# Turned exponentials through memory: where the permutation is done, at the store or at the load

## The chip, the cores and the metric

One core of one Trainium2 chip runs the whole program in one launch. The metric is the device time of an execution in microseconds (us). A profiled execution also has a span: the time from its first to its last recorded instruction. Engine names in the rows are those of the profile: PE is TensorE, PEld its weight loads, DVE is VectorE, ACT is ScalarE, POOL is GpSimd, SP is SyncE. A q behind a name is that engine's queue, where it issues DMAs.

## The reference

The program is local attention followed by a gated feed-forward layer.

```python
# q, k, v: (8, 8, 576, 64); heads 0-3 see a plain window of 32, heads 4-7 every 4th of 128
scores = np.matmul(q, k.transpose(0, 1, 3, 2)) / np.sqrt(64)
scores = np.where(masks[None], scores, -1e9)
attn = np.exp(scores - scores.max(-1, keepdims=True))
attn = attn / (attn.sum(-1, keepdims=True) + 1e-9)
y = np.matmul(attn, v)
# x: the heads of a token side by side, (4608, 512)
g = x @ w_gate                                   # 512 -> 1536
out = (g / (1 + np.exp(-g)) * (x @ w_val)) @ w_out   # 1536 -> 512
```

## The kernel before

**Feed-forward.** The 4608 tokens are nine chunks of 512. The first three go through plain products; the other six are taken two by two (NCS = 3 pairs) through seven products of half-size blocks in place of eight (NT = 7, the names of the loops at lines 1171 to 1206). In each pair a stage of gate and value products comes first (6 blocks of 7 products, each product in two groups of 6 matmuls, one into bank `bg` or a `bo` and one into `bv` or a `bo`), then a stage of output products. Every fp32 operand is split in a high and a low part, so each product takes three matmuls. The mixed weights of the seven products are kept in device memory as `pieces` and come back in loads of 512 KB through a ring of seven (`next_piece`, line 996). A finished product is either kept by ACT (`keep`, line 1071) or summed by DVE (`total`, line 1075), which frees its bank of PSUM.

**Attention.** It is cut in 38 packs (`packs`, line 125). A pack has 2 x 4 x 4 blocks of 32 queries by 64 keys. Its steps run beside the feed-forward work, three visits to a pack, at slots given by `visits` (line 854) and carried out by `attend` (line 878):

- Visit A: the results of an earlier pack (`results`, line 625) and this pack's scores (`scores`, line 552) on TensorE, both into the two banks `two`; then `norm` (line 636) and `turn_y` (line 654) of the earlier pack, and `shift` (line 572) and `exps` (line 589) of this one. Then the loads: keys and queries, values, and, from pack 20 on, `load_far` (line 618) of the pack before.
- Visit B: the exponentials are turned, so that keys lie on partitions. Up to pack 19 TensorE does it (`turn_e`). From pack 20 on (TURNED) `turn_far` (line 610) does it: DVE transposes every block of 32 x 32 into a tile `x`, which is stored to the memory buffer `turned` (two of them, used in turn), and `load_far` loads it into the tile `pt`. The blocks still have to be put in order, 4 by 4, and that is done by the pattern of the transfers.
- Visit C: the results are put where the feed-forward work takes its input (`x_copies`).

For these 18 packs, the exponentials of pack m are stored after its visit B, loaded at visit A of pack m + 1, and used by TensorE at visit A of pack m + 2 (`ended`, line 873).

In the stage of these packs the rings of `later` (line 517) have one buffer each: `e`, `y` and `pt` of one tile each. `norm` writes its result into `y`, and `turn_far` its transposed blocks too.

**What sets the order.** Everything behind the start is recorded by the class Desk (line 155) and issued in an order that Desk.issue plans; the order of TensorE's work stays as written, that of the other engines is planned. Desk.places (line 184) says which blocks of memory an instruction touches: of on-chip memory the columns, without regard to partitions; of a DRAM tile the number of a 128 x 1024 block, which is 0 for all of `turned`. An instruction that writes blocks is planned behind the last writer and the readers of them (`used`, line 209). A DMA is planned with 430 ns at its issue, its bytes at 373 per ns and 2000 ns to land, and counts one instruction behind another as late as that. Its priority is its way, the length of the chain behind it:

```python
    LANDING, RATE, AHEAD = 2000, 373, 2000
    EARLY = 6000
    ...
            cost, later = 430, self.LANDING + nbytes(out) / self.RATE
    ...
            way[k] = cost + later + (self.EARLY if later and e == 'scalar' else 0) + max((way[m] for m in after[k]), default=0)
```

The real waits on the chip are put in by the framework; the plan only gives each engine its order.

Of the kernel before, what the change touches and what calls it, by code (L numbers as in the profile page):

```python
# [34 lines left out]
BQ = 32  # L35
# [40 lines left out]
NH = 4  # L76
# [251 lines left out]
def attention_moe(ctx, tc, qkb, vb, w, const, out):  # L328
    nc = Desk(tc.nc)
# [33 lines left out]
    turned = [tc.dram_tile([P, P * NG], F32, name=f"turned{n}") for n in range(2)]  # L363
# [246 lines left out]
    def turn_far(m, pool):  # L610


        x = pool["y"]()
        e = st[m]["e"].rearrange("q (g b k) -> q b g k", g=NG, b=4)
        nc.vector.transpose(out=x.rearrange("q (b g k) -> q b g k", b=4, g=NG), in_=e)
        nc.sync.dma_start(out=turned[m % 2], in_=x)

    def load_far(m, pool):
        t = pool["pt"]()
        far = turned[m % 2].rearrange("(j k) (b x) -> b k j x", b=4, j=NH)  # L620
        for b in range(4):
            nc.scalar.dma_start(out=t[BQ * b:BQ * b + BQ].rearrange("k (j x) -> k j x", j=NH), in_=far[b])
        st[m]["pt"] = t

    def results(m, two):
# [183 lines left out]
    for n, x in enumerate(MASKS[:4]):  # L809
        nc.vector.tensor_copy(out=mask_sb[:, BK * n:BK * n + BK], in_=two_masks[:, BK * "Fo".index(x):][:, :BK])  # L810
    nc.vector.tensor_copy(out=mask_sb[:, 4 * BK:].rearrange("q (g k) -> q g k", k=BK),
                          in_=two_masks[:, BK:].unsqueeze(1).broadcast_to([P, NM - 4, BK]))
# [65 lines left out]
    def attend(now):  # L878
        for what, m in visit.get(now, ()):
            r = ended(m)  # L880
            if what == "A":
# [14 lines left out]
                if 2 * NSTART <= m < TURNED:  # L896
                    load_v(m, later, nc.sync)
                elif TURNED <= m - 1 < NPK:
                    load_far(m - 1, later)
                    load_v(m - 1, later, nc.sync)  # L900
                if 2 * NSTART <= m + 1 < NPK:
                    load_qk(m + 1, later, nc.sync)
            elif what == "B":
                if TURNED <= m < NPK:
                    turn_far(m, later)
                elif m < NPK:
                    turned_at = bank_o[3] if m == BEFORE - 1 else two[:, 1]
                    turn_e(m, turned_at)
                    keys(m, turned_at, pool_of(m))
            elif r is not None:  # L910
                x_copies(r)
# [342 lines left out]
```

## Time and profile before

| | us |
|---|---|
| median of 3 runs | 910.74 (910.35 to 911.76) |
| the profiled execution | 911.71 |
| its span | 909.9 |
| TensorE busy | 898.7 (99%) |
| DVE busy | 651.9 (72%) |
| ACT busy | 382.3 (42%) |
| POOL busy | 261.0 (29%) |

The granted clock of TensorE has a mean of 0.996 of its full speed. Busy shares are read first, then the waits of the engine that is busiest; matmuls are pipelined and their ends are modelled, so gaps between starts say more than idle time. The 18 stores into `turned` are issued between 333.2 and 656.2 us, the 72 loads from it between 335.7 and 671.2 us. The DMA-issuing instructions of a queue are not counted as busy time of its engine.

### The profile page before, as it was taken

Reading aid. Unit: us, or ns where it says so; the run is one execution under the profiler, and the core shown is the slowest. Engines: PE = TensorE matmul, PEld = TensorE weight load, DVE = VectorE, ACT = ScalarE, POOL = GpSimd, SP = SyncE. Lnnn points to the kernel's source line nnn. Section 1 sums busy time; section 2 is a strip of 40 time slices with the busy share of each in tenths; the row PEclk is TensorE's granted clock in tenths of the full one; section 3 lists DMA queues with packets and bytes.
Section 4 is the critical chain, followed back from the end, with each engine's and each line's share of the span. In section 5 each row is a group of like instructions: output and inputs, shape, how many; then the busy total and the mean of one; then the engine's idle time right before and its main releaser. Section 6 shows DMA issues by size and latency. Waiting matters only on the chain.

```text
span 909.9 us, 20899 instructions
## 1 busy us (share of the span) xinstructions
PE 898.7 (99%) x8642; PEld 737.2 (81%) x8642; DVE 651.9 (72%) x993; ACT 382.3 (42%) x593; POOL 261.0 (29%) x177
## 2 busy tenths in 40 slices
PE   7999999999999999999999999999999999999998
PEld 4988888888888888888888888787878888888886
DVE  6889779978795473777789767878687746555752
ACT  5887423332333242333345533432445533334452
POOL 2479612212211121111132620111046501213451
PEclk9999999999999999999999999999999999999999
DMA  9999976545374641888887778888866675565562
GB/s 347 367 342 343 371 266 236 178 153 181 117 268 143 206 137 39 279 277 275 283 289 263 227 246 296 293 285 270 274 215 217 214 243 192 190 203 186 193 223 93
DMA packets 90382, 214.24 MB, mean 235 GB/s; under 512 B 9264, under 2 KB 32432, under 8 KB 90288
## 3 DMA queue, kind: packets, MB, share of 16 engines
q1 hardware_dynamic: 79776, 208.09, 66.9%
q10 hardware_dynamic: 10512, 4.82, 2.0%
q8 instruction: 68, 1.11, 0.5%
q14 instruction: 26, 0.21, 0.1%
HBM read 165.69 MB, written 47.19 MB: 234 GB/s over the span
## 4 chain that ended last, share of the span: by engine, by line
PE 92%; DMA 4%; DVE 2%; ACT 1%; issue 0%; SPq 0%; ACTq 0%; DVEq 0%
PE bo L251 42%; PE bv L251 22%; PE bg L251 22%; PE two L251 6%; DMA at_float<-turned 2%; DVE at_float L251 1%; DMA at_int<-w 1%; DMA at_float<-qkb 1%; ACT at_int L251 0%; ACT at_float32r L251 0%; SPq L235 0%; DVE at_int L251 0%; DVE at_float32r L251 0%; ACT at_float L251 0%; ACT at_int L235 0%
## 5 line engine op out<-in xcount | busy, mean ns | idle before, releaser
L251 PE MATMUL bo<-at_float32r 128*128 128x512 f32 x1296 | 305.5, 390 | 0.0
L251 PEld LDWEIGHTS bo<-at_float32r 128*128 128x128 f32 x1296 | 242.6, 188 | 50.9
L251 POOL TENSOR_TENSOR at_float32r<-at_float,at_float32r 128x512 fp32r<-128x512 f32 (+1 forms) x109 | 161.3, 1483 | 392.3 <-ACT at_float32r L251 236.2
L251 ACT CAST at_float32r<-at_float 128x512 fp32r<-128x512 f32 (+2 forms) x214 | 147.4, 705 | 162.8 <-DVE at_float L251 72.5
L251 DVE TENSOR_TENSOR at_float<-bo,at_float 128x512 f32<-128x512 f32 x168 | 114.2, 684 | 99.8 <-ACT at_float L251 63.5
L251 DVE TENSOR_TENSOR at_float32r<-at_float,at_float32r 128x512 fp32r<-128x512 f32 (+1 forms) x105 | 109.0, 1052 | 55.2 <-ACT at_float32r L251 43.8
L251 PE MATMUL bv<-at_float32r 128*128 128x512 f32 x486 | 128.5, 391 | 0.0
L251 PE MATMUL bg<-at_float32r 128*128 128x512 f32 x486 | 128.2, 390 | 0.0
L251 ACT ACTIVATE at_float<-at_float 128x512 f32<-128x512 f32 (+1 forms) x108 | 67.9, 630 | 133.4 <-DVE at_float L251 111.9
L251 POOL TENSOR_TENSOR at_float<-at_float,at_float 128x512 f32<-128x512 f32 x36 | 51.2, 1423 | 211.3 <-DVE at_float L251 210.3
L251 PE MATMUL bg<-at_float32r,at_float32r 128*128 128x512 f32 (+1 forms) x468 | 108.9, 381 | 1.5 <-POOL at_float32r L235 0.9
L251 PE MATMUL bv<-at_float32r,at_float32r 128*128 128x512 f32 (+1 forms) x468 | 108.0, 380 | 0.0
L251 DVE SCALAR_TENSOR_TENSOR at_float<-at_float,at_float 128x512 f32<-128x512 f32 x144 | 106.3, 744 | 1.1
L251 PE MATMUL bo<-at_float32r,at_float32r 128*128 128x512 f32 (+1 forms) x468 | 106.5, 376 | 0.0
L251 PEld LDWEIGHTS bg<-at_float32r 128*128 128x128 f32 x486 | 90.9, 188 | 19.1
L251 PEld LDWEIGHTS bv<-at_float32r 128*128 128x128 f32 x486 | 90.7, 188 | 19.2
L251 PEld LDWEIGHTS bg<-at_float32r,at_float32r 128*128 128x128 f32 x468 | 83.2, 190 | 18.7 <-POOL at_float32r L235 1.3
L251 PEld LDWEIGHTS bv<-at_float32r,at_float32r 128*128 128x128 f32 x468 | 83.7, 192 | 16.5 <-DVE at_float L251 0.6
L251 PEld LDWEIGHTS bo<-at_float32r,at_float32r 128*128 128x128 f32 x468 | 82.8, 188 | 16.3
L251 ACT COPY at_float<-bg 128x512 f32<-128x512 f32 x63 | 37.0, 587 | 84.9 <-PE bg L251 81.0
L251 DVE TENSOR_TENSOR at_float<-at_float,at_float 128x512 f32<-128x512 f32 (+2 forms) x80 | 63.9, 808 | 2.4 <-POOL at_float L251 1.2
L251 ACT COPY at_float<-bv 128x512 f32<-128x512 f32 x63 | 37.1, 589 | 36.8 <-PE bv L251 35.3
(74 smaller groups left out, 620.4 us busy)
## 6 DMA issues: line engine op xcount, KB each, us to landing
at_float32r<-pieces SPq DMA_DIRECT2D x189, 512.0 KB, 4.2
pieces<-at_float32r SPq DMA_DIRECT2D x126, 256.0 KB, 4.4
at_float<-qkb SPq DMA_DIRECT2D x32, 576.0 KB, 6.4
at_float<-vb SPq DMA_DIRECT2D x34, 520.0 KB, 5.3
at_int<-w SPq DMA_DIRECT2D x38, 384.0 KB, 6.0
out<-at_float SPq DMA_DIRECT2D x36, 256.0 KB, 4.4
turned<-at_float SPq DMA_DIRECT2D x18, 256.0 KB, 4.7
at_float<-turned ACTq DMA_DIRECT2D x72, 64.0 KB, 5.0
```

What stands on the lines that cost most here:

```text
L251: self.kept.append([engine, lambda: f(*a, **k), sorted(m for m in after if m >= 0), cost, later, both, start])
```

## The change

The store of the transposed tile becomes four stores, one for each group of 32 partitions, which write the blocks of 128 elements where they belong in `turned`. The four loads, one for each group of 32 partitions of `pt`, become one plain load of the whole tile. The bytes are the same: 256 KB each way. The contiguous run is 2048 bytes in the old store and the new load, 512 bytes in the old loads and the new stores. The stores are issued by SP and the load by ACT, as before.

```diff
         x = pool["y"]()
         e = st[m]["e"].rearrange("q (g b k) -> q b g k", g=NG, b=4)
         nc.vector.transpose(out=x.rearrange("q (b g k) -> q b g k", b=4, g=NG), in_=e)
-        nc.sync.dma_start(out=turned[m % 2], in_=x)
+        far = turned[m % 2].rearrange("(b k) (j x) -> j k b x", b=4, j=NH)
+        for j in range(NH):
+            nc.sync.dma_start(out=far[j], in_=x[BQ * j:BQ * j + BQ].rearrange("k (b x) -> k b x", b=4))
 
     def load_far(m, pool):
         t = pool["pt"]()
-        far = turned[m % 2].rearrange("(j k) (b x) -> b k j x", b=4, j=NH)
-        for b in range(4):
-            nc.scalar.dma_start(out=t[BQ * b:BQ * b + BQ].rearrange("k (j x) -> k j x", j=NH), in_=far[b])
+        nc.scalar.dma_start(out=t, in_=turned[m % 2])
         st[m]["pt"] = t
```

## Rows read from the trace of the kernel before

**Rows 1.** Page, part 1: engine, busy us (share of span), instructions.

```profile
PE 898.7 (99%) x8642; PEld 737.2 (81%) x8642; DVE 651.9 (72%) x993; ACT 382.3 (42%) x593; POOL 261.0 (29%) x177
```

**Rows 2.** Busy us (instructions) in stretches; then granted clock, DMA share, GB/s.

```profile
355.00:470.00 115.00, 115.00 (x1292) 94.27 (x1291) 81.53 (x137) 42.24 (x70) 15.59 (x12) 1.00 0.80 265
...
550.00:685.00 135.00, 133.25 (x1605) 108.70 (x1591) 106.48 (x178) 52.24 (x87) 24.24 (x18) 1.00 0.82 270
```

**Rows 3.** Waits of PE, 320 to 680 us: total us, times, longest.

```profile
PE two L251 <- DMA at_float<-turned: 1.8, 4, 0.7
```

**Rows 4.** Timeline of PE, first matmul of six passes and first behind: start, us.

```profile
563.00 0.81 PE L251 MATMUL two<-at_float,at_float 64*32 64x65 f32 x60
...
564.43 0.96 PE L251 MATMUL bo<-at_float32r 128*128 128x512 f32 x3
...
576.89 0.30 PE L251 MATMUL two<-at_float,at_float 64*32 64x65 f32 x2
...
578.94 0.73 PE L251 MATMUL bo<-at_float32r 128*128 128x512 f32 x2
...
619.20 0.30 PE L251 MATMUL two<-at_float,at_float 64*32 64x65 f32 x2
...
621.60 0.96 PE L251 MATMUL bo<-at_float32r 128*128 128x512 f32 x3
...
634.07 0.89 PE L251 MATMUL two<-at_float,at_float 64*32 64x65 f32 x60
...
635.57 0.73 PE L251 MATMUL bv<-at_float32r 128*128 128x512 f32 x2
...
648.04 0.30 PE L251 MATMUL two<-at_float,at_float 64*32 64x65 f32 x2
...
649.89 0.97 PE L251 MATMUL bo<-at_float32r 128*128 128x512 f32 x3
...
662.36 0.30 PE L251 MATMUL two<-at_float,at_float 64*32 64x65 f32 x2
...
663.97 0.98 PE L251 MATMUL bv<-at_float32r 128*128 128x512 f32 x3
```

**Rows 5.** Timeline of ACT, 563 to 573 us (ACTq: DMA issues).

```profile
563.89 0.84 ACTq L251 DMA_DIRECT2D at_float<-turned  x2
...
568.84 0.59 ACT L251 COPY at_float<-bg 128x512 f32<-128x512 f32 x1 [0.59 <-PE bg L251]
568.85 0.31 ACTq L251 DMA_DIRECT2D at_float<-turned  x1
...
572.72 0.31 ACTq L251 DMA_DIRECT2D at_float<-turned  x1
```

**Rows 6.** DMAs, 330 to 680 us: queue's packets, MB, share; issues, KB, us to landing.

```profile
q10 hardware_dynamic: 10368, 4.72, 5.2%
...
turned<-at_float SPq DMA_DIRECT2D x18, 256.0 KB, 4.7
at_float<-turned ACTq DMA_DIRECT2D x72, 64.0 KB, 5.0
```

**Rows 7.** Timeline of SP's queue, 556 to 576 us.

```profile
556.95 0.32 SPq L251 DMA_DIRECT2D turned<-at_float  x1
...
570.72 0.32 SPq L251 DMA_DIRECT2D turned<-at_float  x1
572.91 3.04 SPq L251 DMA_DIRECT2D at_float32r<-pieces  x2
```

**Rows 8.** Timeline of DVE, 581 to 585 us.

```profile
581.08 0.68 DVE L251 TENSOR_TENSOR at_float<-two,at_float 128x512 f32<-128x512 f32 x1
...
582.63 0.69 DVE L251 TENSOR_TENSOR at_float<-bo,at_float 128x512 f32<-128x512 f32 x1
583.68 0.71 DVE L251 STREAM_TRANSPOSE at_float<-at_float 128x512 f32<-128x512 f32 x1 [0.36 <-ACT at_float L251]
```

## Prediction, before any run of the changed kernel

> **What bounds the kernel now.** I read the page's busy shares first: TensorE is busy for nearly the whole span [rows 1]. The table of stretches then says the same of the two stretches where the changed transfers run, 355 to 470 us and 550 to 685 us: the first shows no idle TensorE at all, the second 1.75 us in 135 [rows 2]. So work taken off another engine is worth nothing by itself; only a wait of TensorE can be won. The list of TensorE's waits has one entry there: the passes into `two` waited four times for loads from `turned`, 1.8 us in all [rows 3].
>
> That list counts idle time only, and matmul ends are modelled, so I priced the waits from the timeline by starts. A pass that waits for nothing takes 1.43 us from its first matmul at 563.00 to the first matmul behind it at 564.43 [rows 4]. Five others, all in the second stretch, take 2.05, 2.40, 1.50, 1.85 and 1.61 us [rows 4]. Their excess is 0.62 + 0.97 + 0.07 + 0.42 + 0.18 = 2.26 us. **That is all the change can win.**
>
> Why the loads are late is seen on ACT: two of one pack's loads go out from 563.89, the third at 568.85, the fourth at 572.72 [rows 5]; with the 5.0 us median of such a load [rows 6] the fourth would land at 577.7, and its pass begins at 576.89 [rows 4]. The spreading is the planner's: Desk.places looks at columns, not partitions, so the four loads, which write the same columns of `pt`, count as a chain of writers (0.43 + 2.00 + 0.18 = 2.61 us each, lines 164 and 243), and other ACT work is put between them. The three gaps add up to 572.72 - 563.89 = 8.83 us, 2.94 each.
>
> **The change part by part.** *Four loads become one.* ACT issues three fewer DMAs in each of 18 packs, at 0.31 us each [rows 5], some 17 us of queue time on an engine busy under 40% of these stretches [rows 2]: nothing, since ACT is not what TensorE waits for. The chain of four goes. One load of 256 KB has the store's size, 4.7 us, against 5.0 us for 64 KB [rows 6]; I take 4.7.
>
> *One store becomes four.* SP issues three more DMAs, 3 x 0.32 us a pack [rows 7], beside piece loads that wait for TensorE anyway: 0. Packets of 512 bytes move from the load to the store. The loads' queue shows 10368 packets in 5.2% of 16 engines over 350 us, 28 ns each [rows 6]; 512 of these over 16 engines are 0.9 us, taken off one side and put on the other: 0.
>
> *The chain moves to SP.* To the planner the whole `turned` buffer is one block (line 193), so the four stores now count as a chain of writers, and the load waits for the last. Before shows no such store; the bounds are 0.32 us between stores (issued back to back [rows 7]) and 4.7 us (each waits until the one before has landed [rows 6]). I take 2.94 us, the gap that the same chaining rule gave the loads. It also is close to the 2.72 us between two piece loads on SP (a pair fills 3.04 us, less 0.32 of the second issue [rows 7]), and pieces are what will stand between the stores.
>
> *Does the load come in time?* Take the tightest pack: store at 556.95 [rows 7], pass at 576.89 [rows 4], 19.94 us. After the change: 3 x 2.94 to the last store, 4.7 to its landing, 4.7 for the load: 18.2 us. It lands 1.7 us ahead, so the 2.26 us go. The ends: back to back, 10.4 us, 9.6 us ahead; with 4.7 us gaps 23.5 us, 3.6 us late.
>
> *The wait it adds.* `y` is a single buffer in this stage (line 517): turn_far's transposed tile and norm's result share it. Norm's multiply on DVE ran at 581.08 [rows 8], and the store of 570.72 [rows 7] had landed by 575.4: 5.7 us to spare. The last of four stores goes out at 570.72 + 8.83 = 579.55 and lands at 584.25: the multiply would be held 3.2 us. The planner knows of the dependence and moves the multiply to 579.55 + 2.61 = 582.16 in its plan, so 2.1 us of hold are left. Behind it on DVE stand the total of a bank (582.63) and the next pack's transpose (583.68) [rows 8]; ACT is held likewise at the load, for 2.1 us, with the copies from `bg` and `bv` behind it. Who waits for them? TensorE, when it writes the bank again. After the copy of 568.84, 0.59 us [rows 5], there are three groups of six matmuls (half of 2.72 each) before the bank is due: over 3 us, enough. The tight one is product 4: kept by ACT (0.59), then the total on DVE (0.69 [rows 8]), with one product (2.72) before its bank is written: 1.44 us of margin, once in seven products or 19 us. A 2.1 us hold falls on it in 2.1/19 = 11% of 18 packs, two packs, and costs at most 2.1 - 1.44 = 0.66 us: 0 to 1.3 us, I take 0.6. The lower end is no cost: what follows is then hidden by the margin. A gain is excluded, since nothing here gets `y` earlier.
>
> *Priorities.* The planner adds 6 us of urgency to each ACT load in a chain (line 263). Four chained loads and the store gave 4 x 8.61 + 3.13 = 37.6 us, now it is 4 x 2.61 + 9.13 = 19.6 us. Transposes and exponentials of these packs lose 18 us of urgency and may run a little later on DVE, which has 28 us idle in 135 [rows 2]. TensorE's order is fixed. I take 0 within the 1.7 us that the load is ahead.
>
> *A rule against the split.* The trace shows 64 KB landing no sooner than 256 KB, 5.0 and 4.7 us [rows 6]. The Trainium skill, "DMA: Bandwidth & Descriptors", Rules for kernel authors, asks for one transfer over all partitions, as split ones serialize and small ones are mostly overhead; the trace agrees on the overhead, and no row shows the serializing. By it four stores would follow each other at 4.7 us, the late end above, instead of 2.94.
>
> **The sum.** Of the profiled execution: 911.71 - 2.26 + 0.6 = 910.05, say 910.0 us. That execution is 0.97 us above the median of the runs, 910.74; if this scatter sits in the same waits, the median run has only some 1.3 us of them to lose, and 910.0 is 0.7 us below it, 0.08%. A measurement of this kernel tells about 0.2%, 1.8 us, from no change.
>
> **The rivals.** *All of it is gained.* The scatter lies elsewhere (the start, where transfers bound), every run loses the 2.26 us, and the holds fall on margins: 910.74 - 2.26 = 908.5. For it: the waits have one cause, which goes. Against: it needs the holds to cost nothing. Chance 0.20.
>
> *Nothing is gained.* The waits of the five passes stay or come back, since pieces between the stores push the load out by the 1.7 us: 911.0, the median with the 0.3 us of half a hold. Chance 0.11.
>
> *Slower by the one `y` buffer.* The stores spread so that the multiply is held the full 3.2 us, or more. It decides from the point where a hold passes 1.44 us and meets product 4. At 3.2 us it meets it in 3.2/19, one pack in six, three of 18, costing 1.76 us each, 5.3 us: 909.45 + 5.3 = 914.7. If it met it in every pack, 909.45 + 18 x 1.76 = 941. For it: 581.08 lies ahead of 584.25, and the next pack's transpose, which starts the next chain, is behind the held multiply. Against: DVE has 3 us idle per pack, and the planner sees the dependence. The serialized stores above belong here too: 3.6 us late in nine packs at most, 32 us. Chance 0.23.
>
> **How the numbers follow.** The forecast has the other 0.46. Below 908.9 lies the first rival and a little of the forecast, over 912.6 the last: faster 0.22, same 0.55, slower 0.23. The range goes from just under the full gain, 908.3, to 913.5, which takes in the forecast with its hold at 1.3 us and the lighter part of the slower case; 0.18 is left out.
>
> **What would show it.** In the changed kernel, one ACT issue a pack, at 256 KB, and 72 stores of 64 KB on SP with pieces between them, some 9 us from the first to the last; the five passes back at 1.43 us, and TensorE's waits for `turned` gone. New: DVE idle of 2 to 3 us ahead of norm's multiply, put down to the stores, and ACT held as long at the load. Wrong would be: stores back to back (no hold, the full gain), a pass that still waits for `turned`, or TensorE waiting for a total or a copy by more than 1.3 us in all.

## The result, and the profile after

The changed kernel takes 921.57 us (median of 4 runs, 920.58 to 922.42) against 911.25 us for the kernel before on the same chip: a ratio of 1.0114, 95% interval 1.0096 to 1.0131. It is **slower by some 10 us**, 1.1%. The prediction was 910.0 us with a range of 908.3 to 913.5; it had the sign wrong and the time lies far outside.

The profiled execution took 920.58 us, its span is 918.8 us, 8.9 longer than before. The parts of the page that answer to those of before, engine shares and DMA issues:

```profile
PE 897.6 (98%) x8642; PEld 735.2 (80%) x8642; DVE 664.0 (72%) x993; ACT 380.8 (41%) x593; POOL 261.6 (28%) x177
...
turned<-at_float SPq DMA_DIRECT2D x72, 64.0 KB, 4.2
at_float<-turned ACTq DMA_DIRECT2D x18, 256.0 KB, 5.5
```

TensorE is as busy as before [rows 1]; all the added time is waiting. The table of stretches says where (columns as in [rows 2]):

```profile
355.00:500.00 145.00, 144.69 (x1662) 117.98 (x1661) 108.96 (x176) 57.23 (x95) 26.25 (x19) 1.00 0.82 263
...
550.00:694.00 144.00, 133.94 (x1675) 109.08 (x1674) 104.06 (x177) 52.60 (x89) 23.82 (x18) 1.00 0.81 257
```

In the first stage of the changed transfers TensorE idles 0.31 us, in the second 10.06, against 1.75 before [rows 2]. Together that is 8.6 us more than before, nearly the whole 8.9. The timeline of TensorE in the second stage has four of the five long passes of before at full speed (1.40 to 1.42 us from the first matmul in `two` to the first behind it), as forecast; the fifth, a short pass of 64 matmuls, takes 0.78 us. But there are new waits, one ahead of a product (589.13) and four ahead of passes, where before had none:

```profile
589.13 1.66 PE L251 MATMUL bo<-at_float32r 128*128 128x512 f32 x6 [1.19 <-DVE at_float L251]
...
624.06 0.80 PE L251 MATMUL two<-at_float,at_float 64*32 64x65 f32 x60 [2.68 <-DMA at_float32r<-pieces]
...
641.21 0.80 PE L251 MATMUL two<-at_float,at_float 64*32 64x65 f32 x60 [3.21 <-DMA at_float<-turned]
...
657.63 0.80 PE L251 MATMUL two<-at_float,at_float 64*32 64x65 f32 x60 [2.51 <-DMA at_float<-turned]
...
672.06 0.85 PE L251 MATMUL two<-at_float,at_float 64*32 64x65 f32 x64 [0.47 <-DVE at_float L251]
```

The five make 10.06 us, the idle time of that stretch. The pass at 624.06 is put down to a load of pieces. But by the trace those pieces landed at 624.10, after the pass had begun, and the pass's own load from `turned`, issued at 618.33, landed at 623.92, 0.14 us ahead of it. So this wait is of the same kind as the next two.

Why is the load late? The chain of waits of the changed kernel shows it for the pass at 641.21 (start, us, what):

```profile
631.60 4.10 DMA turned<-at_float
635.70 0.02 issue
635.72 5.36 DMA at_float<-turned
641.07 0.14 issue
641.21 1.48 PE two L251 x86
```

The last of the four stores goes out at 631.60, lands 4.1 us later, and only then the load starts. The first of these four stores had gone out at 621.16; SP's queue shows what stood between:

```profile
621.16 0.32 SPq L251 DMA_DIRECT2D turned<-at_float  x1
621.57 0.38 SPq L251 DMA_DIRECT2D at_float32r<-pieces  x1
624.94 0.33 SPq L251 DMA_DIRECT2D at_float<-vb  x1
625.33 0.42 SPq L251 DMA_DIRECT2D turned<-at_float  x1
625.84 1.56 SPq L251 DMA_DIRECT2D at_float<-qkb  x1
628.51 0.32 SPq L251 DMA_DIRECT2D at_float32r<-pieces  x1
628.88 0.43 SPq L251 DMA_DIRECT2D turned<-at_float  x1
631.23 0.32 SPq L251 DMA_DIRECT2D at_float32r<-pieces  x1
631.60 0.42 SPq L251 DMA_DIRECT2D turned<-at_float  x1
```

Stores alternate with loads of pieces, which follow TensorE's products (2.72 us from the one at 628.51 to the next), and the second store stands behind the load of values (`vb`). In this stage `vb` goes out some 0.9 us after the start of each pass, here the late one at 624.06. From the first store to the last it is 10.44 us. DVE shows the other side, norm's multiply held for the stores in `y`:

```profile
587.07 0.69 DVE L251 TENSOR_TENSOR at_float<-two,at_float 128x512 f32<-128x512 f32 x1 [3.21 <-DMA turned<-at_float]
587.79 0.71 DVE L251 STREAM_TRANSPOSE at_float<-at_float 128x512 f32<-128x512 f32 x1
588.43 0.65 DVE L251 TENSOR_TENSOR at_float<-bo,at_float 128x512 f32<-128x512 f32 x1
589.68 0.71 DVE L251 STREAM_TRANSPOSE at_float<-at_float 128x512 f32<-128x512 f32 x1 [0.60 <-ACT at_float L251]
...
602.81 0.69 DVE L251 TENSOR_TENSOR at_float<-two,at_float 128x512 f32<-128x512 f32 x1 [1.70 <-DMA turned<-at_float]
...
618.26 0.69 DVE L251 TENSOR_TENSOR at_float<-two,at_float 128x512 f32<-128x512 f32 x1 [2.80 <-DMA turned<-at_float]
```

The transpose at 589.68 makes the next pack's tile. The product at 589.13 waits for the sum at 588.43, which stands behind the held multiply. Before, a pack's first store went out 6 to 8 us ahead of the following pass; in the changed kernel 6.06, 5.15, then 3.02, 2.35, 2.90, 3.28, 3.07 and 1.22 us ahead (2.90 is the store at 621.16 ahead of the pass at 624.06). The stores lose half of their lead within three packs; behind that the lead stays near 3 us only because the passes now wait as well.

### The profile page after: what moved, and what is told of

Its sections match the earlier page's. It is cut to its first block, busy times and chain, and to the rows that moved or that the text cites. A ratio compares the mean times of both kernels' runs of the same rounds, so it can differ in the third digit from the quotient of the medians.

```text
span 918.8 us, 20861 instructions
## 1 busy us (share of the span) xinstructions
PE 897.6 (98%) x8642; PEld 735.2 (80%) x8642; DVE 664.0 (72%) x993; ACT 380.8 (41%) x593; POOL 261.6 (28%) x177
## 4 chain that ended last, share of the span: by engine, by line
PE 90%; DMA 7%; DVE 2%; SPq 1%; issue 0%; ACT 0%; DVEq 0%; ACTq 0%
PE bo L251 41%; PE bv L251 22%; PE bg L251 21%; PE two L251 6%; DMA at_int<-w 2%; DMA turned<-at_float 2%; DMA at_float<-turned 1%; DMA at_float<-qkb 1%; DVE at_float L251 1%; DMA at_float<-vb 1%; DMA at_float32r<-pieces 1%; SPq L251 0%; DVE at_float32r L251 0%; SPq L235 0%; DVE at_int L251 0%
## 5 line engine op out<-in xcount | busy, mean ns | idle before, releaser
L251 DVE TENSOR_TENSOR at_float32r<-at_float,at_float32r 128x512 fp32r<-128x512 f32 (+1 forms) x105 | 120.2, 1161 | 45.0 <-ACT at_float32r L251 36.4
L251 PEld LDWEIGHTS bo<-at_float32r,at_float32r 128*128 128x128 f32 x468 | 82.8, 188 | 16.3
L251 DVE TENSOR_TENSOR at_float<-at_float,at_float 128x512 f32<-128x512 f32 (+2 forms) x80 | 66.7, 841 | 1.2 <-ACT at_float L251 1.2
```

Source lines behind the costliest of these rows:

```text
L251: self.kept.append([engine, lambda: f(*a, **k), sorted(m for m in after if m >= 0), cost, later, both, start])
```

## The experiments

**Theory "loop through y".** The planner chains the four stores, SP spreads them, the last one lands late. It holds norm's multiply in the one `y`; behind it stand the next pack's transposes, which write `y` too, so the next four stores begin later. One turn of this loop is longer than the 13.9 us between two passes of the second stage, and the lag grows until loads come late. **Rivals:** the 512-byte permuting stores are slow in themselves ("writes"); the load behind a late last store is enough without `y` ("late load"); each further store costs its share ("any chain").

**Stores back to back.** In Desk.places:

```diff
                     blocks = ap.offset // (P * PIECE),
+                    if t.name.startswith("turned"):
+                        whole = int(np.prod([n for _, n in ap.ap])) == P * P * NG
+                        blocks = (0, 1, 2, 3) if whole else (ap.offset // P % 4,)
```

> The changed kernel, but the planner is told that the four stores write different parts of the buffer, so it issues them back to back on SP. Theory 'spread' (the loss comes from the plan, which chains the four stores and lets loads of pieces, values and keys in between, so that the last one lands late): the last store goes out about 1.3 us after the first instead of 7 to 10 us, the waits of 1.3 to 3.3 us ahead of the passes go, 908.5 to 911 us. Theory 'writes' (512-byte permuting stores are slow in themselves, or fill the transfer engines): still 918 or more, with landings of the stores well over 5 us.

Measured 908.87 us (9 runs, 908.59 to 909.26), ratio to the kernel before 0.9975 (0.9966 to 0.9985). SP's queue and the stretch of the second stage:

```profile
583.89 1.77 SPq L254 DMA_DIRECT2D turned<-at_float  x4
...
655.13 1.76 SPq L254 DMA_DIRECT2D turned<-at_float  x4
```

```profile
550.00:685.00 135.00, 135.00 (x1632) 110.65 (x1618) 108.63 (x183) 54.69 (x91) 24.50 (x19) 1.00 0.83 275
```

The four leave one right behind the other, and TensorE has no idle time left in the stage. The same permuting stores, the same plain load: the whole loss is gone and the forecast gain is there. "Writes" falls.

**Plain stores, same chain.** In turn_far of the changed kernel:

```diff
-            nc.sync.dma_start(out=far[j], in_=x[BQ * j:BQ * j + BQ].rearrange("k (b x) -> k b x", b=4))
+            nc.sync.dma_start(out=turned[m % 2][BQ * j:BQ * j + BQ], in_=x[BQ * j:BQ * j + BQ])
```

> The changed kernel with four stores that do not permute (each writes 32 whole rows of 2048 bytes; the blocks then lie in the wrong order, so the attention of these packs is wrong), same chain in the plan. Theory 'spread': as slow as the changed kernel, 918 to 923 us, since the plan is the same. Theory 'writes': the 512-byte runs were the cost, 909 to 912 us.

Measured 920.36 us (917.03 to 921.48), ratio 1.0092 (1.0073 to 1.011). With runs of 2048 bytes the loss stays, and the multiplies are held as in the changed kernel:

```profile
586.07 0.69 DVE L251 TENSOR_TENSOR at_float<-two,at_float 128x512 f32<-128x512 f32 x1 [3.62 <-DMA turned<-at_float]
601.53 0.69 DVE L251 TENSOR_TENSOR at_float<-two,at_float 128x512 f32<-128x512 f32 x1 [1.41 <-DMA turned<-at_float]
617.86 0.69 DVE L251 TENSOR_TENSOR at_float<-two,at_float 128x512 f32<-128x512 f32 x1 [3.42 <-DMA turned<-at_float]
```

The permutation is not the cost; the chain of four is.

**A tile of its own.** The stores stay spread, but turn_far no longer writes `y`:

```diff
-        x = pool["y"]()
+        x = at(M_LATE + 11 * CS, TP) if TURNED < m != 29 else pool["y"]()
```

> The changed kernel, stores spread as in it, but turn_far writes its transposed tile into a buffer of its own (16 of 18 packs) instead of y. Theory 'one buffer' (the late last store costs time only because norm's multiply waits for it in the one y and pushes the next pack's transposes back, pack after pack): DVE's waits for the stores go, the lag no longer grows, 909.5 to 913 us. Theory 'late load' (the load behind the late last store is enough): passes still wait for the load, 915 to 921 us. Theory 'writes': 918 or more.

Measured 909.14 us (907.83 to 910.36), ratio 0.9983 (0.9973 to 0.9992), a little under the 909.5 expected of theory 'one buffer'. A pack of it in SP's queue, as spread as in the changed kernel:

```profile
583.78 0.32 SPq L251 DMA_DIRECT2D turned<-at_float  x1
...
585.98 0.44 SPq L251 DMA_DIRECT2D turned<-at_float  x1
...
588.70 0.44 SPq L251 DMA_DIRECT2D turned<-at_float  x1
...
591.84 0.33 SPq L251 DMA_DIRECT2D at_float<-vb  x1
592.22 1.64 SPq L251 DMA_DIRECT2D turned<-at_float  x1
```

The last store goes out 8.44 us after the first and stands behind `vb`, the load follows at 13.84 us, and no pass waits: the first store is 7.16 us ahead of its pass here, and the load has until the pass after that, 21.03 us behind the first store. DVE's waits for the stores fall from 12.7 us to 1.0 (list of waits, 320 to 700 us, the changed kernel and then this one):

```profile
DVE at_float L251 <- DMA turned<-at_float: 12.7, 6, 3.2
```

```profile
DVE at_float L251 <- DMA turned<-at_float: 1.0, 1, 1.0
```

So a late last store alone costs nothing. "Late load" falls; the shared tile is needed. The tile of its own also takes the shared `y` out of the plan, so that norm's multiply comes earlier in DVE's order as well: for the passes from 549.32 to 646.44 it starts 3.1 to 6.4 us after its pass here. In the changed kernel it starts 9.0 to 11.7 us after it for the passes from 578.04 to 657.63, and the stores hold only 0.8 to 3.2 us of that on the chip. This run does not tell the share of the wait on the chip from that of the later place in the plan; both come from the one `y`.

**Where the lag is made.** The same tile in one stage only: `TURNED < m < 29` for the first, `m > 29` for the second.

> The changed kernel with a tile of its own for the transposed blocks in the first stage alone (packs 21 to 28, passes 15.3 us apart). Theory 'loop through y': the loss is made in the second stage, where passes are 13.9 us apart, so this stays as slow as the changed kernel, 917 to 922 us. If the lag were carried over from the first stage, it is near 909 us.

> The same tile in the second stage alone (packs 30 to 37, passes 13.9 us apart). Theory 'loop through y': the whole loss goes, 908.5 to 910.5 us, although stores stay spread and y stays shared in the first stage. If the first stage makes part of the loss, 912 us or more.

The first measured 920.13 us (917.75 to 922.76), ratio 1.01 (1.0075 to 1.0124); the second 909.25 us (907.67 to 912.04), ratio 0.9979 (0.9969 to 0.999). All of the loss is made in the second stage. In the first, where most passes are some 15.3 us apart, stores are as spread and `y` is as shared, and at most 0.4 us is lost (row of the second kernel). That the longer period is the reason is argued: no run changes the period alone.

```profile
355.00:500.00 145.00, 144.60 (x1663) 118.19 (x1663) 108.86 (x175) 56.57 (x93) 26.54 (x19) 1.00 0.81 260
```

**Two stores in the chain.** Two of 64 whole rows in place of four:

```diff
-        far = turned[m % 2].rearrange("(b k) (j x) -> j k b x", b=4, j=NH)
-        for j in range(NH):
-            nc.sync.dma_start(out=far[j], in_=x[BQ * j:BQ * j + BQ].rearrange("k (b x) -> k b x", b=4))
+        for j in range(2):
+            nc.sync.dma_start(out=turned[m % 2][D * j:D * j + D], in_=x[D * j:D * j + D])
```

> The changed kernel with two stores of 64 whole rows in place of four that permute (the blocks then lie in the wrong order, so the attention of these packs is wrong); chained in the plan as the four are. Theory 'loop through y' (the time from the first store to the landing of the last, plus the multiply and two transposes, must be under the 13.9 us between two passes of the second stage): the last store goes out some 3 us after the first and lands by 8 us, before the multiply is due at 10, so there is no hold and no lag, 908.5 to 910.5 us. Theory 'any chain costs' (each further store costs a third of the loss of the four): a third of 10 us, 913 to 915 us.

Measured 908.33 us (906.91 to 908.95), ratio 0.9972 (0.996 to 0.9983), 0.2 us under the range expected of the loop. The second store follows the first by 1.1 to 2.7 us in the second stage:

```profile
569.11 0.62 SPq L251 DMA_DIRECT2D turned<-at_float  x1
...
571.79 0.45 SPq L251 DMA_DIRECT2D turned<-at_float  x1
```

No loss at all, not a third of it: the cost is not a price per store but sets in somewhere between two chained stores and four (three were not run). "Any chain" falls.

**Nobody permutes, one store and one load.** The four lines above become `nc.sync.dma_start(out=turned[m % 2], in_=x)`.

> One plain store and one plain load, nobody permutes (the attention of these packs is wrong): the floor of this change. 908.5 to 909.3 us, all passes 1.42 us. If the changed kernel with its stores back to back measures the same, the four permuting stores cost nothing of their own.

Measured 908.72 us (907.73 to 909.97), ratio 0.9977 (0.9968 to 0.9986). It is the same as four permuting stores issued back to back (0.9975), so with the stores issued one right behind the other no run shows a cost of the permutation.

**The loads of before, unchained.** The planner is told that they write different partitions of `pt`:

```diff
                     blocks = tuple(np.unique(at * size // 32).tolist())
+                    if t.name == self.by_rows:
+                        a = ap.offset // ap.ap[0][0]
+                        blocks = tuple((x, r) for x in blocks for r in range(a // BQ, (a + ap.ap[0][1] - 1) // BQ + 1))
```

> The kernel before (one store, four loads), but the planner is told that the four loads write different partitions, so it issues them one behind the other. If the five long passes of before (2.26 us) come from the planner's chain of loads, all passes take 1.42 us and the time is 908.0 to 909.5 us, 1.5 to 2.3 under before. If they come from the transfers themselves, it stays within 0.5 us of before.

Measured 909.13 us (908.6 to 911.19), ratio 0.9981 (0.9971 to 0.999). A pack's four loads now leave together:

```profile
564.20 1.80 ACTq L255 DMA_DIRECT2D at_float<-turned  x4
```

All passes with scores and results take 1.42 us, and the two last ones, with results alone, 0.79. The five long passes of before were the planner's chain of loads, and the kernel before can have this gain without the change.

**Both cures.**

> Both cures together: stores back to back and a buffer of their own. If each cure alone already takes all waits of the passes away, this gives the same as either alone, 908.5 to 909.5 us. If each leaves a rest that the other takes, it is below 908.5 us.

Measured 908.51 us (907.72 to 909.41), ratio 0.9975 (0.9965 to 0.9985): the same as the stores back to back alone. Neither cure leaves a wait that the other takes.

## Why the prediction was wrong

- **What can be won, 2.26 us:** right in its cause, too small for the execution that it was read from. The pass at 662.36 is a short one, of 64 matmuls; one that waits for nothing takes 0.79 us (677.84 to 678.63 below), not 1.43, so its excess is 0.82 us and not 0.18, and the sum is 2.90. The profiled execution with stores back to back took 908.85 us, 2.86 under that of before. By the medians the kernels in which no pass waits are 1.6 to 2.2 us under the kernel before.

```profile
663.20 0.84 PE L251 MATMUL two<-at_float,at_float 64*32 64x65 f32 x62 [0.54 <-DMA at_float<-turned]
...
677.84 0.86 PE L251 MATMUL two<-at_float,at_float 64*32 64x65 f32 x64
678.63 0.73 PE L251 MATMUL bg<-at_float32r 128*128 128x512 f32 x2
```

- **The planner chains the stores, 2.94 us between them:** right. 3 x 2.94 = 8.8 us was forecast from the first to the last; in the second stage it is 6.8 to 10.6 us. The load was to start at 13.5 us; it starts at 10.9 to 14.6.
- **512-byte runs cost nothing:** right, by the plain stores (as slow as the permuting ones) and by the kernel that doesn't permute (as fast as they are back to back).
- **The multiply is held, 2.1 us:** right in kind and size, six holds of 2.1 us in the mean (12.7 us in the list of waits); three more multiplies (463.32, 478.76, 570.61) start within 0.2 us of a last store's landing and wait 0.5 to 1.4 us, listed under other names. For banks that come late by the holds 0.6 us was taken, 1.3 at most. It is 1.19 us, ahead of the product at 589.13, and at most 1.5 with a wait of 0.31 at 484.35, which was not traced to a hold.
- **"It lands 1.7 us ahead":** this is the step that failed. The 18.2 us from the first store to the landing of the load were sized well: it takes 16.9 to 19.9 us in the seven packs whose stores begin from 558.06 to 654.57 (the load itself takes 5.5 us at the median where 4.7 was taken). What was wrong is the 19.94 us that this has. They were read from before, where nothing delays the first store. But by the next paragraph the next pack's transpose is behind the held multiply, and the next first store is behind that transpose. I counted the hold as a one-off, once per pack, against the margins of the banks (0.6 us), and not as a delay that the next pack inherits. With a lead of 2.4 to 3.3 us and 13.9 us to the next pass, 16.3 to 17.2 us are left to the third pack and the four behind it.

  One turn of the loop measures, from the store at 621.16: 10.44 us to the last store, 4.10 to its landing at 635.70, 2.23 for the multiply and the transposes to the next first store at 637.93, 16.77 us in all, where passes ought to come every 13.9. Over the five turns from 590.42 to 670.84 a turn takes 16.1 us, against 14.2 for the same packs with stores back to back (583.89 to 655.13): 5 x 1.83 = 9.2 us, most of the 10.06 that TensorE waits in the stage. Already the first turn, from 558.06 to 572.89, takes 14.83 us, before any pass is late; from 621.16 on the second store stands behind `vb`, which comes with the late pass, and the chain, 7.3 us at first, takes as much as 10.6. In the first stage most passes are 15.3 us apart and the chain is 6 to 9 us, and there the loop closes in time.

```profile
558.06 0.32 SPq L251 DMA_DIRECT2D turned<-at_float  x1
...
572.89 0.32 SPq L251 DMA_DIRECT2D turned<-at_float  x1
...
590.42 0.32 SPq L251 DMA_DIRECT2D turned<-at_float  x1
...
637.93 0.32 SPq L251 DMA_DIRECT2D turned<-at_float  x1
...
670.84 0.32 SPq L251 DMA_DIRECT2D turned<-at_float  x1
```

```profile
635.72 0.69 DVE L251 TENSOR_TENSOR at_float<-two,at_float 128x512 f32<-128x512 f32 x1 [0.77 <-DMA turned<-at_float]
636.45 1.46 DVE L251 STREAM_TRANSPOSE at_float<-at_float 128x512 f32<-128x512 f32 x2
```

- **The slower rival** named the right place, the one `y`, at 0.23, and even the link, the next transpose behind the held multiply. Its price, 5.3 us, was mis-sized for the same reason: it priced holds that make a bank late for TensorE (1.5 us at most, above), and not the lag.
- **The other long price, stores that wait for each other's landing**, and the rule of the Trainium skill beside it ("DMA: Bandwidth & Descriptors", Rules for kernel authors: split transfers serialize): no run shows stores that follow each other at 4.7 us. Stores back to back go out within 1.3 to 2.4 us, land in 3.5 us at the median, and in the second stage the four of a pack land within 0.7 us of each other in all packs but the last (2.6). What spread them was the plan.
- **The scatter of the runs:** forecast as sitting in the same waits; the runs leave it open. The kernel before ranges from 908.73 to 913.0 us in 25 runs beside the first experiments, the one with stores back to back from 908.59 to 909.26 in 9. But the kernel with the tile of its own in the second stage, in which no pass waits either, ranges from 907.67 to 912.04.

## What to carry to other kernels

When a transfer out of a shared buffer gets later, follow the buffer round to the next time it is filled, and compare that loop with the period of the work. Here the delay was free where passes came every 15.3 us, and added up where they came every 13.9 and a turn took 16.1. A distance read from the trace of before holds only as long as nothing in the change moves its first end. And where a planner decides, look at what it believes about the pieces: the same four stores cost 10 us or win 2, by whether it knows that they don't overlap. Last, a pass that waits is to be compared with one of its own kind: the short pass at 662.36 hid 0.6 us of what could be won.

## What was not expected of the hardware

The issue itself of a small store took long in places: the 64 KB store at 579.94 held SP's queue for 2.91 us, behind the loads of values and of keys and queries just issued, and landed 6.95 us after its issue. These loads alone do not explain it, as the store at 609.33, behind the same two, took 0.42 us; the cause stays open.

```profile
578.93 0.33 SPq L251 DMA_DIRECT2D at_float<-vb  x1
579.55 0.33 SPq L251 DMA_DIRECT2D at_float<-qkb  x1
579.94 2.91 SPq L251 DMA_DIRECT2D turned<-at_float  x1
```

And one plain load of 256 KB landed no sooner than a quarter of it had: 5.5 us at the median in the changed kernel, where 4.7 was taken, against 5.0 for 64 KB [rows 6].
